# A Nyström attention with a SiLU layer behind it, on one core: landmarks spread in another slot, second-layer matmuls ahead of two groups of scores, batch 3's maximum by VectorE, and the first period and a load of v reordered

## The chip, the cores and the metric

The kernel runs on one core of a Trainium2 chip. The metric is the device time of one execution in microseconds. It uses TensorE (PE in the profile), VectorE (DVE), ScalarE (ACT), GpSimd (POOL) and SyncE (SP, which only issues DMAs here). GpSimd issues the loads of q, k, v and of both weights; SyncE issues the output stores and the DMA transposes.

## The reference

Eight batches, eight heads, 576 tokens, head size 64. q and k are averaged over 18 neighbouring tokens to 32 landmarks a head. Three softmax matrices are made, a pseudo-inverse of the middle one is iterated, and the product goes through a two-layer network with SiLU:

```python
def sm(a, b):
    s = scale * np.matmul(a, b.transpose(0, 1, 3, 2))
    s = s - np.max(s, axis=-1, keepdims=True)
    e = np.exp(s)
    return e / (np.sum(e, axis=-1, keepdims=True) + 1e-09)
A = sm(q, k_lm)
Bm = sm(q_lm, k_lm)
C = sm(q_lm, k)
Z = Bm.transpose(0, 1, 3, 2) / (norm1(Bm) * norminf(Bm) + 1e-06)
for _ in range(6):
    Z = 2 * Z - Z @ Bm @ Z
attn = A @ Z @ C @ v
x = attn, heads side by side: (4608, 512)
h = x @ w_in                      # 512 to 2048
g = h * (1.0 / (1.0 + np.exp(-h)))
out = g @ w_out                   # 2048 to 512
```

## The kernel before

The order of the work is written out by hand: each engine runs its instructions in the order of the program, and waits only on semaphores.

**Loops.** After a prologue that does batch 0's attention, an outer loop goes over the batches b = 0 to 7, one "period" each. Within it run 16 slots, s = 0 to 15. In every slot TensorE does one step of the first layer for batch b (`l1`, four matmuls into a PSUM tile `hps`), ScalarE applies SiLU to it and writes `gT` (`act`), and TensorE then does some matmuls of the second layer (`l2_mm(n)`, group `ops`, 512 columns each, 16 to a tile of 128 tokens), from a queue of finished token tiles. How many is listed by slot: `CNT[0]` and `CNT[1]` for loops 0 and 1, `REST` for loops 2 to 7. Each period needs 72 of them. Whenever 16 are done, ScalarE copies the tile to `ost` and SyncE stores it.

**Attention of the next batch.** Between these steps loop b does the attention of batch b+1 (object `a` of class `Att`; `a0` is that of batch b). It starts in slot d, which is 2, 3, 0 for loops 0, 1 and the rest. The methods that matter here:

- `lm_t` (line 251): VectorE transposes the landmarks `lmn` to `lmc`. `bd_expand` (line 259): four GpSimd copies spread the landmarks of k from `lmc` into the block-diagonal `bd`, which A's scores read. `transpose_qk` (line 185): VectorE transposes one quarter of q and k to `qkT`; the scores read it. `landmarks_pool` (line 211 on): GpSimd sums the landmarks of batch b+2 in slots 4 and 8 of loops 2 to 5.
- `a_scores(i)`: TensorE makes A's scores for token chunks 2i and 2i+1 into a PSUM bank `sa`. `a_max(i)` (line 568): VectorE takes the maximum of each row and head, `nm`.
- Two ways to take off the maximum. Where `sub` is set (batches 4 to 7), `a_sub(i)` (line 581) has VectorE write `xs` = scores - maximum to SBUF, and one exponential, `a_exp_all` (line 589), does all five chunks. Elsewhere `a_shift(i)` has TensorE add the maximum to the scores in PSUM by one matmul, and `a_exp(i)` (line 594) does the exponentials from PSUM in three parts.
- `b_scores`, `b_max`, `b_exp` for the 32 by 32 matrix in `bb`; `c_scores`, `c_max`, `c_exp` for C in two banks `scp`. These two come from the same two PSUM buffers as `hps`, so that a first-layer step after C waits until the exponential or the activation before it has read its buffer.
- `f_mm`, `b_scale`, `f_out`, `ns_mm`, `ns_step`, `x_out`: the iteration for Z. `w_mm` (reads v and the transposed exponentials of C), `z_mm`, then `m_unit` or `m_pair`: the product with w_in, copied to `mb`, which the first layer of the next loop reads.

`psa` (tiles `sa`, `mp`, `atp`, `wp`, `zt`) has one bank, `pso` (`ops`, `mp`, `ctp` and others) two, `psh` (`hps`, `scp`, `mpp`) two tiles of two banks. ScalarE has to load another table to go from SiLU to the exponential and back (line 151); both changes lie in slots d+1 and d+2.

**The places of the change, before.** At the end of loops 2 to 5 slot 13 has an `m_pair` whose casts VectorE does, slot 14 the last `transpose_qk` and behind it `lm_t` and `bd_expand` for batch b+2. Slot 15 then makes that batch's first scores, maximum and subtraction, though their first reader comes one loop later:

```python
if s == (14 if b > 1 else 15):
    ready = Att(b + 2)
    ready.lm_t(0, 2)
    ready.bd_expand(0, 2, nc.gpsimd.tensor_copy)
if s == 15 and ready.sub:
    ready.a_first()
    ready.a_scores(0)
    ready.a_max(0)
    ready.a_sub(0)
```

In loop 0 the loads are issued in the order four blocks of `w_out`, then v of batch 1 in slot 0, then q and k of batch 2. The first token tile of the second layer starts in slot 4; its 16 matmuls read the four blocks of `w_out` in turn, four matmuls a block. v of batch 1 is read by `w_mm` in slot 8.

Of the kernel before, what the change touches and what calls it, by code (L numbers as in the profile page):

```python
# [40 lines left out]
def kernel(  # L41
# [9 lines left out]
    nc = tc.nc  # L51
    B, H, S, Dh = q.shape
    L = 32
# [55 lines left out]
    def load_v(b):  # L109
        vt = loadp.tile([VP, H, VC * Dh], BF, tag="v", name="v")  # L110
        nc.gpsimd.dma_start(out=vt, in_=v[b].rearrange("h (p c) d -> p h (c d)", c=VC))
        v_t[b] = vt
# [21 lines left out]
    def load_w_out(j):  # L134
        nc.gpsimd.dma_start(  # L135
            out=w_out_sb[:, 4 * j:4 * j + 4, :],
            in_=moe_w_out[512 * j:512 * j + 512, :].rearrange("(c p) m -> p c m", p=128))
# [88 lines left out]
    class Att:  # L226
        def __init__(self, b):
            self.b = b
            self.qkT, self.v, self.lmn = qkT_t[b], v_t[b], lmn_t[b]
            self.bd = bd_t[b % 2]  # L230


            self.tiled = b < 2
            self.by_dma = b >= 2

            self.sub = b >= 4

            self.mean = b <= 2

            self.split = SPLIT[b]  # L240
            self.lmc = attp.tile([128, 4, L, 2], BF, tag="lmc", name="lmc")
            self.bb = None
            self.m_done = 0
            self.csum = attp.tile([128, 2], FP, tag="csum", name="csum")
            self.eCT, self.t = [None, None], [None, None]
            self.s, self.sa, self.w = [None, None], [None] * 3, [None, None]
            self.fx = None
# [79 lines left out]
        def b_scale(self):  # L327
            cs = attp.tile([128, 2], FP, tag="cs", name="cs")
            nc.vector.tensor_reduce(out=cs, in_=self.bmt, op=OP.add, axis=AX.X)
            n1 = attp.tile([128, 2], FP, tag="n1", name="n1")  # L330
            nc.vector.tensor_reduce(out=n1, in_=cs.unsqueeze(2).to_broadcast((128, 2, L)),
                                    op=OP.max, axis=AX.X, apply_transpose=True)
            self.nrm = attp.tile([128, 2], FP, tag="nrm", name="nrm")
            w = self.fw
            self.fx = nsp.tile([128, 2, w + L], BF, tag=f"fx{w}", name="fx", bufs=3)
            if self.tiled:
                nc.vector.tensor_scalar(out=n1, in0=n1, scalar1=1e-6, scalar2=-1.0, op0=OP.add,
                                        op1=OP.mult)
                nc.vector.reciprocal(out=self.nrm, in_=n1)
                nc.vector.tensor_tensor(  # L340
                    out=self.fx[:, :, w:w + L], in0=self.bm,
                    in1=self.nrm.unsqueeze(2).to_broadcast((128, 2, L)), op=OP.mult)
                return
            nc.vector.tensor_scalar(out=n1, in0=n1, scalar1=1e-6, scalar2=None, op0=OP.add)
            nc.vector.reciprocal(out=self.nrm, in_=n1)
            for g in range(2):
                nc.vector.tensor_scalar(out=self.fx[:, g, w:w + L], in0=self.bm[:, g, :],
                                        scalar1=self.nrm[:, g:g + 1], scalar2=None, op0=OP.mult)
# [380 lines left out]
    def l2_mm(n):  # L729

        st = l2_state
        while n > 0 and st["queue"]:
# [16 lines left out]
                nc.sync.dma_start(out=out[r0:r0 + 128, :], in_=ost)  # L749


    CNT = {0: [0, 0, 0, 0, 4, 4, 4, 2, 4, 2, 2, 2, 2, 2, 2, 2],
           1: [2, 2, 2, 2, 2, 6, 8, 8] + [4, 3] * 4}
    REST = [4, 2, 14, 11, 3, 3, 3, 3, 4, 4, 4, 3, 4, 3, 4, 3]


    ORD = (1, 0, 3, 2)
# [8 lines left out]
    a = Att(0)  # L766
# [60 lines left out]
    a.ns_mm(last=True)  # L827
    a.x_out()
    load_w_out(2)
    load_w_out(3)  # L830
    at = ps2("atp")
    a.z_mm(at[:, 1, :])
# [13 lines left out]
    ready = None  # L846
    for b in range(B):
        nxt = b + 1 < B
        cnt = CNT.get(b, REST)
        h = {}  # L850
        a0 = a
        a, ready = ready, None
# [9 lines left out]
        for s in range(NDC):  # L862
# [3 lines left out]
            if s <= d and b < 2:  # L866
# [16 lines left out]
                if b == 0:  # L883
                    transpose_qk(1, ORD[s])
                    if s == 0:
                        load_v(1)
                        a = Att(1)
                    elif s == 1:
                        a.lm_t(0)
                else:  # L890
                    if s == 3:
                        landmarks_out(2, lp, 0, 4)
                        a = Att(2)
                        a.lm_t(0, 2)
                        a.bd_expand(0, 2, nc.gpsimd.tensor_copy)
                    transpose_qk(2, (1, 3, 0, 2)[s])
                l2_mm(cnt[s])
            elif not nxt or s == d:
# [1 line left out]
                act(s)  # L900
                l2_mm(cnt[s])
                if nxt and a.sub:
                    a.a_scores(1)
                    a.a_max(1)
                    a.a_sub(1)

            elif s == d + 1:
                l1(s)
                act(s)
                l2_mm(cnt[s])  # L910
                if b == 0:

                    transpose_qk(1, ORD[s])
                    a.lm_t(1)
                    a.bd_expand(0, 2, nc.gpsimd.tensor_copy)
                    for i in (1, 2):
                        a0.a_scores(i)
                        a0.a_max(i)
                a.b_scores()
                a.c_scores()  # L920
                if a.sub:
                    a.a_scores(2)
                a.b_max()
                a.c_max(0)
# [6 lines left out]
            elif s == d + 2 and a.sub:  # L931
                a.a_start()
                a.c_max(1)
                a.a_max(2)
                a.a_sub(2)
                a.c_exp(0)
                a.c_exp(1)
                a.a_exp_all()
                a.b_norm()
                l2_mm(cnt[s])  # L940
                table(AF.Silu)
                l1(s)
            elif s == d + 2:
                n = cnt[s]
# [19 lines left out]
                a.a_shift(2)  # L964
                a.a_exp(2)
                if b == 0:
                    a0.m_unit(2, nc.vector.tensor_copy, nc.scalar.copy)
                    a.f_mm()
                    a.b_scale()
                    a.f_out()  # L970
                    l2_mm(n)
                    a0.m_unit(3, nc.vector.tensor_copy, nc.vector.tensor_copy)
                else:
                    l2_mm(n - 4 - min(n - 4, 6))
                table(AF.Silu)
                l1(s)
            elif b == 0:
                l1(s)
                r = s - d
                if r == 3:  # L980
                    act(s - 1)
                    a.ns_mm()
                    a.c_transpose(0)
                    a.ns_step()
                    a.c_out(0, nc.scalar.copy)
                    a0.a_norm(1)
                    a0.a_norm(2)
                elif r == 4:
                    a.ns_mm()
                    a.c_transpose(1)  # L990
                    a.w_scale()
                    a.ns_step()
                    a.ns_mm()
                    a.c_out(1)
                    a.a_norm(0)
                    a0.a_transpose(1)
                    a0.a_out(nc.scalar.copy)
                elif r == 5:
                    a.ns_step()
                    a.ns_mm()  # L1000
                    a.a_norm(1)
                elif r == 6:
                    a.w_mm()
                    a.ns_step()
                    a.ns_mm()
                    a.w_out()
                    a.ns_step()
                    a.a_norm(2)
                elif r == 7:
                    a.ns_mm(last=True)  # L1010
                    a.x_out()
                    a.a_transpose(0)
                    a.a_out(nc.scalar.copy)
                elif r == 8:
                    a.z_mm(psa1("zt"))
                    a.z_out()
                    a.a_transpose(1)
                    a.a_out(nc.vector.tensor_copy)
                act(s)
                if r in (9, 11):  # L1020
                    a.m_pair(r - 9)
                l2_mm(cnt[s])
            elif s == d + 3:
                l1(s)
                act(s - 1)
# [49 lines left out]
            if b == 0:  # L1075
                if s == 4:
                    load_qk(2)
                elif s == 11:
                    load_qk(3)
                    load_v(2)  # L1080
            elif b + 2 < B:
                if s == (5 if b == 1 else 1) and b + 3 < B:
                    load_qk(b + 3)
                if s == 7 + d // 2:
                    load_v(b + 2)
                if s in (4 + d, 8 + d):
                    landmarks_pool(b + 2, (s - 4 - d) // 2)

                ts = (9, 10, 12, 14) if d == 0 else (10, 11, 12, 13)
                if s in ts:  # L1090
                    transpose_qk(b + 2, ORD[ts.index(s)])
                if s == (14 if b > 1 else 15):
                    ready = Att(b + 2)
                    ready.lm_t(0, 2)
                    ready.bd_expand(0, 2, nc.gpsimd.tensor_copy)
                if s == 15 and ready.sub:
                    ready.a_first()
                    ready.a_scores(0)
                    ready.a_max(0)
                    ready.a_sub(0)  # L1100
# [35 lines left out]
```

## Time and profile before

| what | value |
|---|---|
| median of three runs | 271.88 us (271.57 to 273.46) |
| profiled execution | 271.72 us, its span 269.9 us |
| TensorE busy | 256.3 us, 95% of the span |
| ScalarE busy | 172.6 us, 64% |
| VectorE busy | 159.7 us, 59% |
| GpSimd busy | 118.0 us, 44% |
| granted TensorE clock | 1.000 |
| second-layer matmuls (`ops`) | 576, 146.3 us |
| first-layer matmuls (`hps`) | 512, 82.5 us |

The span runs from the first instruction to the last; the rest of the execution's time lies around it. Loop 0 begins near 22.8 us, loop 1 near 54.5, loop 2 near 83.3, and each later one about 29.5 us after the one before; after loop 7 the last second-layer matmuls run from 254 to 266 us. In the rows of the timeline the columns are the start and the length in us, the engine, the line, the operation, the tiles written and read with their shapes, and in brackets how long the engine had been idle and what released it. An instruction's recorded length overlaps with its successor's on TensorE, so the rate is read from the starts or from the chain of waits.

### The profile page before, as it was taken

Reading aid. Unit: us, or ns where it says so; the run is one execution under the profiler, and the core shown is the slowest. Engines: PE = TensorE matmul, PEld = TensorE weight load, DVE = VectorE, ACT = ScalarE, POOL = GpSimd, SP = SyncE. Lnnn points to the kernel's source line nnn. Section 1 sums busy time; section 2 is a strip of 40 time slices with the busy share of each in tenths; the row PEclk is TensorE's granted clock in tenths of the full one; section 3 lists DMA queues with packets and bytes.
Section 4 is the critical chain, followed back from the end, with each engine's and each line's share of the span. In section 5 each row is a group of like instructions: output and inputs, shape, how many; then the busy total and the mean of one; then the engine's idle time right before and its main releaser. Section 6 shows DMA issues by size and latency. Waiting matters only on the chain.

```text
span 269.9 us, 6751 instructions
## 1 busy us (share of the span) xinstructions
PE 256.3 (95%) x2761; PEld 144.5 (54%) x2761; DVE 159.7 (59%) x392; ACT 172.6 (64%) x319; POOL 118.0 (44%) x169
## 2 busy tenths in 40 slices
PE   6899898999999999999998999899999999999994
PEld 2647554475555565555645565455545565555541
DVE  4768893549596767586785678586777664000000
ACT  2367966759648856678475956687576857635511
POOL 8515426114897089535964289308950030100000
PEclk9999999999999999999999999999999999999999
DMA  6999999965994955679197918213481612121122
GB/s 101 202 209 207 207 206 219 206 120 97 218 108 88 210 119 77 136 134 180 23 135 138 210 61 122 88 32 107 52 163 39 101 53 71 39 80 39 39 78 78
DMA packets 37790, 32.34 MB, mean 120 GB/s; under 512 B 18816, under 2 KB 29056, under 8 KB 37760
## 3 DMA queue, kind: packets, MB, share of 16 engines
q0 software_dynamic: 15104, 18.35, 42.2%
q1 hardware_dynamic: 22656, 13.57, 21.8%
q8 instruction: 21, 0.34, 0.5%
q14 instruction: 9, 0.07, 0.1%
HBM read 36.70 MB, written 9.44 MB: 171 GB/s over the span
## 4 chain that ended last, share of the span: by engine, by line
PE 75%; DMA 9%; DVE 8%; POOL 3%; issue 2%; ACT 1%; POOLq 0%; ACTq 0%
PE ops L77 41%; PE hps L77 20%; DMA v<-in_v_dram 7%; PE sa L77 3%; PE bb L77 3%; PE scp L77 2%; DVE mb L687 2%; PE mp L77 2%; DMA nat<-in_q_dram 2%; DVE qkT L185 2%; POOL bd L259 2%; PE lmp L77 1%; PE wp L77 1%; DVE nm L568 1%; POOL w_out_sb L135 1%
## 5 line engine op out<-in xcount | busy, mean ns | idle before, releaser
L77 PE MATMUL ops<-w_out_sb,gT 128*128 128x512 bf16 x576 | 146.3, 379 | 0.0
L721 ACT ACTIVATE gT<-hps 128x576 bf16<-128x576 f32 (+2 forms) x128 | 82.5, 650 | 61.8 <-PE hps L77 60.8
L77 PE MATMUL hps<-AT,mb 128*128 128x288 bf16 (+2 forms) x512 | 82.5, 286 | 0.0
L77 PEld LDWEIGHTS <-gT 128*128 128x128 bf16 x576 | 53.0, 98 | 47.1 <-issue 5.4
L77 PEld LDWEIGHTS <-mb 128*128 128x128 bf16 x512 | 48.0, 98 | 24.3 <-issue 0.9
L185 DVE STREAM_TRANSPOSE qkT<-nat 128x576 f32<-128x576 f32 x32 | 39.1, 1245 | 1.5 <-DMA nat<-in_k_dram 1.1
L620 POOL TENSOR_TENSOR an<-ex,arec 128x512 bf16<-128x512 bf16 (+2 forms) x24 | 21.1, 902 | 21.4 <-DVE arec L610 17.9
L747 ACT COPY ost<-ops 128x512 f32<-128x512 f32 x36 | 21.0, 584 | 13.7 <-PE ops L77 13.5
L384 DVE SCALAR_TENSOR_TENSOR fx<-fx,bb 128x320 bf16<-128x320 bf16 (+1 forms) x39 | 17.1, 438 | 18.0 <-PE bb L77 17.3
L211 POOL TENSOR_TENSOR lma<-nat 128x1152 f32<-128x1152 bf16 x10 | 23.7, 2374 | 0.0
L687 DVE CAST mb<-mp 128x512 bf16<-128x512 f32 x28 | 18.0, 685 | 9.7 <-PE mp L77 9.5
L151 ACT ACT_TABLE_LOAD x16 | 20.5, 1283 | 1.1 <-PEq L1120 0.8
L1033 POOL CAST gate<-fx 128x2 f32<-128x2 bf16 x6 | 1.1, 187 | 45.6 <-DVE fx L354 45.6
L568 DVE TENSOR_REDUCE nm<-sa 128x16 bf16<-128x512 f32 (+2 forms) x21 | 12.7, 622 | 11.2 <-PE sa L77 11.1
L259 POOL COPY bd<-lmc 32x128 bf16<-32x128 bf16 (+1 forms) x32 | 8.9, 279 | 21.6 <-DVE lmc L251 15.6
L77 PEld LDWEIGHTS <-qkT 128*128 128x128 bf16 (+1 forms) x160 | 9.9, 98 | 9.7 <-issue 5.7
L77 PEld LDWEIGHTS <-fx 32*32 32x32 bf16 (+1 forms) x168 | 8.3, 93 | 12.0 <-DVE fx L384 1.8
L688 ACT CAST mb<-mpp 128x1024 bf16<-128x1024 f32 x14 | 14.2, 1011 | 0.6 <-PE mpp L77 0.6
L77 PE MATMUL sa<-bd,qkT 128*128 128x128 bf16 (+1 forms) x148 | 11.7, 220 | 2.9 <-POOL bd L259 2.2
L605 DVE TENSOR_REDUCE arec<-ex 128x16 f32<-128x512 bf16 (+2 forms) x24 | 14.1, 587 | 0.1
L77 PE MATMUL bb<-fx 32*32 32x64 bf16 (+2 forms) x168 | 13.1, 205 | 0.4
L425 DVE TENSOR_REDUCE cmx<-scp 128x1 f32<-128x576 f32 x16 | 11.9, 753 | 1.0 <-PE scp L77 0.7
(110 smaller groups left out, 259.1 us busy)
## 6 DMA issues: line engine op xcount, KB each, us to landing
out_dram<-ost SPq DMA_DIRECT2D x36, 256.0 KB, 2.3
nat<-in_k_dram POOLq DMA_DIRECT2D x16, 288.0 KB, 6.5
nat<-in_q_dram POOLq DMA_DIRECT2D x16, 288.0 KB, 7.8
v<-in_v_dram POOLq DMA_DIRECT2D x8, 576.0 KB, 7.2
w_in_sb<-in_moe_w_in_dram POOLq DMA_DIRECT2D x4, 512.0 KB, 15.8
w_out_sb<-in_moe_w_out_dram POOLq DMA_DIRECT2D x4, 512.0 KB, 14.5
AT<-an SPq DMA_TRANSPOSE x30, 4.2
eCT<-eC SPq DMA_TRANSPOSE x12, 4.3
```

Of the source, the lines that this page charges most:

```text
L77: nc.tensor.matmul(out=o, lhsT=lhsT, rhs=rhs, start=start, stop=stop, skip_group_check=True)
L151: nc.scalar.activation(out=spare[:, 1:2], in_=spare[:, 0:1], func=func)
L185: nc.vector.transpose(out=o.rearrange("p (l t) -> p t l", t=SEG), in_=nat_t[b][:, j, :].bitcast(FP).rearrange("p (t l) -> p t l", l=L))
L211: nc.gpsimd.tensor_tensor(out=a1, in0=nat[:, :, 0:3 * w], in1=nat[:, :, 3 * w:6 * w], op=OP.add)
L259: copy[h % len(copy)](out=self.bd[p, g:g + n, 32 * h:32 * h + 32, :], in_=self.lmc[p].rearrange("p (g j) l e -> p g j l e", j=2)[:, g:g + ...
L384: nc.vector.scalar_tensor_tensor(out=n, in0=self.fx, scalar=2.0, in1=self.p, op0=OP.mult, op1=OP.add if self.tiled else OP.subtract)
L568: eng.tensor_reduce(out=self.nm[0:pr, c:c + n, :], in_=self.sa[i][0:pr, 0:256 * n].rearrange("p (c h l) -> p c h l", h=8, l=L), op=OP.max, ...
L620: nc.gpsimd.tensor_tensor(out=self.an[0:pr, c:c + n, :].rearrange("p c (h l) -> p (c h) l", l=L), in0=x, in1=r.unsqueeze(2).to_broadcast(( ...
L687: nc.vector.tensor_copy(out=o[:, r, 0:512], in_=m[r])
L688: nc.scalar.copy(out=o[:, :, 512:1024], in_=m2)
L721: nc.scalar.activation(out=gT_t[b][:, 2 * s:2 * s + 2, o + c0:o + c1], in_=h[:, :, 0:c1 - c0], func=AF.Silu)
L747: nc.scalar.copy(out=ost, in_=st["ps"])
```

## The change

It has five parts.

- In loops 2 to 5, `Att(b+2)`, `lm_t` and `bd_expand` move from slot 14, behind the last transpose, to slot 13, ahead of it.
- `REST` puts more second-layer matmuls ahead of A's second scores (5 for 4) and ahead of B's and C's scores (4 for 2), and fewer behind (12 for 14, 10 for 11).
- Batch 3 now has `sub`: VectorE takes its maximum off. A new flag `early` keeps for batches 4 to 7 what is done in the loop before; batch 3's three groups of scores, maxima and subtractions stand in slots 0, 1 and 2 of loop 2, the last behind the first four second-layer matmuls of slot 2.
- In loop 0, slot 4, the four second-layer matmuls come first, then `f_mm` with `b_scale` ahead of it, then `m_unit(2)` and `m_unit(3)`, one right behind the other. In slot 10 the two second-layer matmuls move ahead of `a_transpose(1)`. `CNT[0]` takes two matmuls out of slot 6 and puts two into slot 9.
- The load of v for batch 1 is issued between the third and the fourth block of `w_out`.

```diff
-            self.sub = b >= 4
+            self.sub = b >= 3
+
+            self.early = b >= 4
...
-            w = self.fw
+            w = self.fw = L if self.tiled else 128
...
-    CNT = {0: [0, 0, 0, 0, 4, 4, 4, 2, 4, 2, 2, 2, 2, 2, 2, 2],
+    CNT = {0: [0, 0, 0, 0, 4, 4, 2, 2, 4, 4, 2, 2, 2, 2, 2, 2],
            1: [2, 2, 2, 2, 2, 6, 8, 8] + [4, 3] * 4}
-    REST = [4, 2, 14, 11, 3, 3, 3, 3, 4, 4, 4, 3, 4, 3, 4, 3]
+    REST = [5, 4, 12, 10, 3, 3, 3, 3, 4, 4, 4, 3, 4, 3, 4, 3]
...
     load_w_out(2)
+    load_v(1)
     load_w_out(3)
...
                     if s == 0:
-                        load_v(1)
                         a = Att(1)
...
                 if nxt and a.sub:
-                    a.a_scores(1)
-                    a.a_max(1)
-                    a.a_sub(1)
+                    i = 1 if a.early else 0
+                    if i == 0:
+                        a.a_first()
+                    a.a_scores(i)
+                    a.a_max(i)
+                    a.a_sub(i)
 
             elif s == d + 1:
                 l1(s)
                 act(s)
                 l2_mm(cnt[s])
+                if a.sub and not a.early:
+                    a.a_scores(1)
+                    a.a_max(1)
+                    a.a_sub(1)
...
                 a.b_scores()
                 a.c_scores()
-                if a.sub:
+                if a.early:
                     a.a_scores(2)
...
             elif s == d + 2 and a.sub:
                 a.a_start()
                 a.c_max(1)
+                if not a.early:
+                    l2_mm(4)
+                    a.a_scores(2)
                 a.a_max(2)
                 a.a_sub(2)
...
-                l2_mm(cnt[s])
+                l2_mm(cnt[s] if a.early else cnt[s] - 4)
                 table(AF.Silu)
                 l1(s)
...
                 if b == 0:
+                    a.b_scale()
+                    l2_mm(n)
+                    a.f_mm()
+                    a.f_out()
                     a0.m_unit(2, nc.vector.tensor_copy, nc.scalar.copy)
-                    a.f_mm()
-                    a.b_scale()
-                    a.f_out()
-                    l2_mm(n)
                     a0.m_unit(3, nc.vector.tensor_copy, nc.vector.tensor_copy)
...
                 elif r == 8:
                     a.z_mm(psa1("zt"))
                     a.z_out()
+                    l2_mm(cnt[s])
                     a.a_transpose(1)
...
-                l2_mm(cnt[s])
+                l2_mm(cnt[s] if r != 8 else 0)
...
+                if s == 13 and b > 1:
+                    ready = Att(b + 2)
+                    ready.lm_t(0, 2)
+                    ready.bd_expand(0, 2, nc.gpsimd.tensor_copy)
                 ts = (9, 10, 12, 14) if d == 0 else (10, 11, 12, 13)
                 if s in ts:
                     transpose_qk(b + 2, ORD[ts.index(s)])
-                if s == (14 if b > 1 else 15):
+                if s == 15 and b == 1:
                     ready = Att(b + 2)
                     ready.lm_t(0, 2)
                     ready.bd_expand(0, 2, nc.gpsimd.tensor_copy)
-                if s == 15 and ready.sub:
+                if s == 15 and ready.early:
                     ready.a_first()
                     ready.a_scores(0)
```

## The prediction

> **What bounds the kernel now.** I read first the page's busy times and its two lines of slices, then the list of waits, then the timeline around each place that the diff touches. A stretch over one batch period says who sets the pace:
>
> ```profile
> PE 256.3 (95%) x2761; PEld 144.5 (54%) x2761; DVE 159.7 (59%) x392; ACT 172.6 (64%) x319; POOL 118.0 (44%) x169
> PEclk9999999999999999999999999999999999999999
> 114.40:143.90 29.50, 28.79 (x304) 16.21 (x301) 21.40 (x50) 20.11 (x35) 18.48 (x25) 1.00 0.75 120
> ```
>
> TensorE is busy 28.79 of 29.50 us at full clock. It takes its instructions in order, so nothing but its own work and its own idle gaps counts. The waits name the gaps:
>
> ```profile
> PE sa L77 <- POOL bd L259: 2.2, 4, 0.6
> PE sa L77 <- DVE xs L581: 0.6, 4, 0.2
> PE wp L77 <- DMA v<-in_v_dram: 0.5, 1, 0.5
> ```
>
> The first two occur once in each of four periods, the third once, in the first period. One of the four, around 114 us (columns: start, length):
>
> ```profile
> 112.41 0.28 DVE L251 STREAM_TRANSPOSE lmc<-lmn 128x128 f32<-128x128 f32 x1
> 112.70 0.81 PE L77 MATMUL ops<-w_out_sb,gT 128*128 128x512 bf16 x3
> 112.75 1.27 POOL L259 COPY bd<-lmc 32x128 bf16<-32x128 bf16 x4 [2.79 <-DVE lmc L251]
> 114.07 0.62 PE L77 MATMUL sa<-bd,qkT 128*128 128x128 bf16 x8 [0.56 <-POOL bd L259]
> 115.02 1.03 PE L77 MATMUL ops<-w_out_sb,gT 128*128 128x512 bf16 x4
> 115.45 0.69 DVE L581 TENSOR_TENSOR xs<-sa,nm 128x512 f32<-128x512 f32 x1
> 116.20 0.64 PE L77 MATMUL sa<-bd,qkT 128*128 128x128 bf16 x8 [0.16 <-DVE xs L581]
> 118.93 3.18 PE L77 MATMUL ops<-w_out_sb,gT 128*128 128x512 bf16 x14
> 121.39 1.28 ACT L589 ACTIVATE ex<-xs 128x1280 bf16<-128x1280 f32 x1
> 124.56 1.17 ACT L721 ACTIVATE gT<-hps 128x576 bf16<-128x576 f32 x2
> 125.56 0.65 PE L77 MATMUL hps<-AT,mb 128*128 128x288 bf16 x4
> ```
>
> An "ops" matmul takes 0.216 us (fourteen advance the chain by 3.02). Three from 112.70 end at 113.35; A's first scores start at 114.07, 0.72 late, 0.05 after the last bd copy. Four from 115.02 end at 115.88; A's second scores start at 116.20, 0.32 late, because their one PSUM bank is free only when xs ends at 116.14.
>
> **Part a, the landmarks spread in slot 13.** Transpose and four copies (0.28 + 1.27 us) now stand ahead of the last q/k transpose (1.25 us) instead of behind it. VectorE ends its casts of mb in slot 13 at 111.40, so lmc is ready at 111.6, bd at 112.95 and the transpose at 112.8, both before 113.35. The copies now run beside a transpose. The trace has this: at 61.05 four copies took 1.28 us while a transpose at 60.85 took 1.22. GpSimd's queue has nothing between (its landmark sums end at 109.96; the loads of the next period stay behind). All 0.72 goes, four times: -2.9. If the cover is gone: 0.
>
> **Part b, the new counts in loops 3 to 6.** Loops 2 to 7 get 5, 4, 12 and 10 second-layer matmuls in slots 0 to 3 instead of 4, 2, 14 and 11: no work more or less. Take the moment of A's first scores as T (114.07 above). One more ahead of A's second scores fills 0.22 of the 0.32; they stay at T+2.13. Two more ahead of B's and C's scores put these 0.43 later, less the 0.13 that the second score bank now waits for a Silu activation: 0.30. Two fewer behind make the next first-layer step 0.13 earlier, one fewer after that puts the step of slot 4 at 125.56 - 0.13 - 0.22 = 125.21, which is 0.35 gained, if its PSUM bank is free. That bank is freed by the activation that starts at 124.56 and ends 0.65 later, at 125.21. ScalarE works without a pause up to it, from the exponentials through two table loads. Queued behind C's later scores are VectorE's maxima and the last subtraction: xs ends at 121.29 + 0.30 = 121.59, so the big exponential starts at 121.64 instead of 121.39, and with it the output copy, the table load and the activation come 0.25 later: 125.46. The step then starts at 125.50 instead of 125.56. I take -0.06 a batch, -0.2 in four, and keep -0.35 a batch (ScalarE not late) and +0.2 (twice as late) as ends: -1.4 to +0.8. In loop 7 no scores stand between; 0.
>
> **Part c, batch 3's maximum by VectorE (loop 2).** Gone are three TensorE matmuls that add the shift (0.216, 0.216 and 0.11 us by their columns: 0.54); three exponentials (1.57) become one of 1.28. New are three subtractions by VectorE (0.69, 0.69, 0.42). A's first scores move from behind C's scores to slot 0. In before the period runs so:
>
> ```profile
> 84.33 1.03 PE L77 MATMUL ops<-w_out_sb,gT 128*128 128x512 bf16 x4
> 94.68 1.17 ACT L721 ACTIVATE gT<-hps 128x576 bf16<-128x576 f32 x2
> 96.04 0.65 PE L77 MATMUL hps<-AT,mb 128*128 128x288 bf16 x4
> ```
>
> Five "ops" from 84.33 put T at 85.41 (bd is there at 84.96). From T on VectorE does what it does in the four later batches: maximum, subtraction, maximum, subtraction (to T+4.2), B's and C's maxima, maximum, subtraction (to T+7.2), as 121.29 stands to 114.07. The big exponential starts then, and the activation that frees the bank ends 3.8 later, at T+11.1, as 125.21 stands to 114.07. That is 96.5; the step starts at 96.55 instead of 96.04. TensorE itself would be there at about 95.6, so its saving of 0.54 ends in a wait of about 0.9 us. C's exponentials, and SP's transposes of them, come about 2.4 us later too; at the page's 4.3 us to landing they are there by 97, and w, their reader, came at 99.17. I take +0.5. Ends: -0.5 if ScalarE were no limit, +1.2 if its whole delay (94.68 to 95.9) came through.
>
> **Part d, the first period.** The page's queue of weights and v is served in order of issue, about 2.5 us each: the four w_out blocks are issued at 20.44 to 22.71 and land at 32.26 to 39.88 (11.8 and 17.2 us on), v, issued at 23.52, lands 19.3 later at 42.8. With v ahead of the last w_out block, v lands at 40.3 and the block at 42.8. The block's first reader is the 13th second-layer matmul; the counts 4, 4, 2, 2, 4 put that into slot 8, behind w.
>
> ```profile
> 33.34 0.22 PE L77 MATMUL bb<-bmt 32*32 32x32 bf16 x8 [0.34 <-ACT ex L594]
> 36.27 0.49 PE L450 MATMUL ctp<-ident,eC 128*96 128x128 bf16 x6 [0.26 <-DVE mb L667]
> 42.85 0.56 PE L77 MATMUL wp<-v,eCT 96*32 96x64 bf16 x48 [0.50 <-DMA v<-in_v_dram]
> 47.27 0.64 PE L642 MATMUL atp<-ident,an 128*128 128x128 bf16 x4 [0.45 <-DVE zwT L518]
> ```
>
> Slot 4: the four "ops" now fill the wait for the exponentials, f keeps its start at 33.34 (it reads the bank that they release), and both m units come behind it at 33.49. But the second of them waits for the copies of the first, done at 34.63, where before it stood behind the "ops": it ends at 35.0 instead of 34.8, and C's transpose comes at 36.48 instead of 36.27. So 0.2 is lost, and slots 5 to 7 run 0.2 late with two "ops" fewer (0.43). w then starts at 41.9, its v long there, ends at 42.4, and the "ops" behind wait for the w_out block: 42.86, against 43.51 before, with two still owed in slot 9: 0.65 - 0.43 = 0.2 gained. In slot 10 two "ops" now stand in the 0.6 us between z and A's transpose; that hides 0.5. Sum -0.7; ends -1.2 (both waits gone, nothing lost) and +0.3 (the lost 0.2, a late block, nothing hidden).
>
> **Sum.** The profiled execution took 271.72 us (span 269.9, 1.8 around it), 0.16 under the median of the runs. -2.9 - 0.2 + 0.5 - 0.7 = -3.3; 271.88 - 3.3 = 268.6, rounded to **268.5**.
>
> **Rivals.**
>
> *ScalarE's chain costs more.* In loops 2 to 6 my step of slot 4 hangs on an estimate of VectorE's and ScalarE's queue to a tenth. For it: two table loads of 1.28 us lie in it, and b starts with no slack. Against it: ScalarE is only 64% busy and has room after. At 0.4 us more in each of five: 270.5.
>
> *TensorE alone sets it.* If exponentials and activations keep up, b gives 1.4 and c gives 0.5 instead of costing it: 271.88 - 2.9 - 1.4 - 0.5 - 0.7 = 266.4. Against it: the activations at 124.56 have no idle time named before them.
>
> *GpSimd and VectorE shut each other out, slower than before.* The bd copies start just as the last transpose would, in slots 13 and 14. If the copies hold the transpose back until 112.95, it ends at 114.2, and A's first scores, which need it too, start at 114.25 instead of 114.07: a turns from -2.9 into +0.7, and the sum is 272.2. It decides from 0.55 us of delay (112.8 to 113.35) on. Against it: the overlapping copies and transpose at 61 us were as long as alone, and a cast at 83.75 too. The Trainium skill, "SBUF — State Buffer", section "Who interferes with whom", knows such an exclusive lock between the two engines, which would give this time; it names copies, casts and scalar forms in two-port modes and operations with two SBUF inputs, and an operation with one input outside those modes is said not to contend. By that the transposes are safe, and the trace's 1.22 us agrees.
>
> *The move does nothing*, since the scores also need the last transpose: they would wait for it at 112.8, still before 113.35; part of the lock's chance.
>
> **How the numbers follow.** Forecast 0.60 (267.6 to 269.6), ScalarE's chain 0.19, TensorE alone 0.14, lock 0.07. The range 266.8 to 270.5 leaves out half of TensorE alone, half of ScalarE's chain and the lock, 0.2 or a little more. About 1%, 2.7 us, is what a measurement of this kernel can tell from no change; that line is 269.2. Faster by more: 0.14 and most of the forecast, 0.66. Slower by more than 1% needs the lock and ScalarE's chain together: 0.04. The rest: 0.30.
>
> **What would show it.** Right: no wait of sa for bd; sa's second wait near 0.1; first-layer steps of slot 4 waiting for an activation, about 0.9 us in loop 2 and 0.3 in loops 3 to 6; no wait of w for v, and one of "ops" for a w_out block at 42.8; periods of loops 3 to 5 near 28.7 us instead of 29.5. Wrong: bd or the transposes longer than 1.3 us, a wait of sa for qkT, or a period unchanged though sa no longer waits.

## The result, and the profile after

The changed kernel takes **269.38 us** (median of 6 runs, 268.52 to 270.85), the kernel before 272.19 in the 6 runs beside it: a ratio of 0.990, with a 95% interval of 0.9865 to 0.9935. Forecast were 268.5, and 266.8 to 270.5 as the range. The profiled execution took 269.39 us, its span is 267.4.

The page's line of busy times, and the same stretch as before, one period of loop 3 (columns: length, then busy time and instructions of PE, PEld, DVE, ACT and POOL, the clock, the share and rate of the DMAs):

```profile
PE 250.0 (93%) x2718; PEld 143.4 (54%) x2758; DVE 161.6 (60%) x395; ACT 173.4 (65%) x317; POOL 118.0 (44%) x169
```

```profile
114.00:142.74 28.74, 28.04 (x300) 16.15 (x302) 21.46 (x50) 20.24 (x35) 19.08 (x26) 1.00 0.80 133
```

The period is 28.74 us instead of 29.50, at the same clock, and TensorE still fills it. (Its total on the page is lower than it was, but the trace of this execution holds 2718 matmuls beside 2758 weight loads, so some forty are missing and the totals are not to be subtracted; the lengths of periods are.) The list of waits has lost its entry of "sa" for "bd" and that of "wp" for v. Of the two lines below the first is nearly the same as before, the second is new:

```profile
PEld L77 <- DVE xs L583: 2.7, 6, 0.6
PE hps L77 <- ACT gT L723: 2.1, 5, 0.7
```

The second line says that five times in the run a first-layer step waits for an activation, 0.7 us at most. (The step of slot 3 in loop 2 also waits, 0.20 us, for an exponential of C.) The first is a weight load that waits ahead of A's scores; it stands beside matmuls that are still running, so most of its 2.7 us costs nothing. The timeline around the beginning of loop 3 (columns: start, length; the line numbers are two higher than before):

```profile
111.64 0.30 DVE L253 STREAM_TRANSPOSE lmc<-lmn 128x128 f32<-128x128 f32 x1
111.86 1.22 DVE L185 STREAM_TRANSPOSE qkT<-nat 128x576 f32<-128x576 f32 x1
112.00 1.27 POOL L261 COPY bd<-lmc 32x128 bf16<-32x128 bf16 x4 [1.78 <-DVE lmc L253]
113.67 0.62 PE L77 MATMUL sa<-bd,qkT 128*128 128x128 bf16 x8
115.06 0.69 DVE L583 TENSOR_TENSOR xs<-sa,nm 128x512 f32<-128x512 f32 x1
115.80 0.64 PE L77 MATMUL sa<-bd,qkT 128*128 128x128 bf16 x8
121.25 1.27 ACT L591 ACTIVATE ex<-xs 128x1280 bf16<-128x1280 f32 x1
124.42 1.17 ACT L723 ACTIVATE gT<-hps 128x576 bf16<-128x576 f32 x2
125.10 0.65 PE L77 MATMUL hps<-AT,mb 128*128 128x288 bf16 x4 [0.27 <-ACT gT L723]
```

The copies of bd now run beside the last transpose, end at 113.27, and A's first scores at 113.67 wait for nothing. The second still start 2.13 after the first, as before, because their bank is free only when xs ends at 115.75; but the matmul that was put ahead of them now fills that wait up to about 0.1 us, too little for a bracket in the list. Further on the step of slot 4 waits 0.27 us, until the first of the two activations at 124.42 has given its bank back.

**Where the time went.** Below is the time from loop to loop, from the first-layer step of slot 0 to the next one, in the profiled execution of every kernel of this study. "Start" is the first of these steps, the end of the prologue; after loop 7's start every kernel takes 38.5.

| kernel | start | loop 0 | 1 | 2 | 3 | 4 | 5 | 6 | span |
|---|---|---|---|---|---|---|---|---|---|
| before | 22.76 | 31.73 | 29.34 | 30.70 | 29.52 | 29.52 | 29.53 | 28.34 | 269.9 |
| after | 23.49 | 30.96 | 29.34 | 30.34 | 28.73 | 28.73 | 28.73 | 28.54 | 267.4 |
| part a alone | 24.07 | 31.15 | 29.34 | 29.97 | 28.80 | 28.81 | 28.81 | 28.34 | 267.8 |
| without part c | 24.14 | 31.27 | 29.71 | 29.98 | 28.73 | 28.73 | 28.73 | 28.27 | 268.1 |
| part d alone | 23.25 | 30.97 | 29.34 | 30.70 | 29.53 | 29.53 | 29.53 | 28.33 | 269.7 |
| C's scores sooner | 23.27 | 30.97 | 29.34 | 30.34 | 28.59 | 28.59 | 28.58 | 28.31 | 266.5 |
| best version | 22.70 | 30.65 | 29.34 | 29.97 | 28.59 | 28.59 | 28.59 | 28.13 | 265.1 |
| batch 3's first scores sooner | 22.77 | 30.96 | 29.34 | 30.06 | 28.73 | 28.73 | 28.73 | 28.55 | 266.4 |
| two copies added | 22.92 | 30.96 | 29.34 | 30.35 | 28.73 | 28.73 | 28.74 | 28.27 | 266.6 |

In the kernel before loop 2 begins at 83.83, so half a microsecond after the 83.3 given above. From before to after the loops give -0.77, 0, -0.36, -0.79, -0.79, -0.80 and +0.20, in all -3.3. The start takes 0.73 back, so the two spans differ by 2.5 only.

### The profile page after: what moved, and what is told of

The parts are those of the page before. It is cut to its first block, busy times and chain, and to the rows that moved or that the text cites. A ratio compares the mean times of both kernels' runs of the same rounds, so it can differ in the third digit from the quotient of the medians.

```text
span 267.4 us, 6703 instructions
## 1 busy us (share of the span) xinstructions
PE 250.0 (93%) x2718; PEld 143.4 (54%) x2758; DVE 161.6 (60%) x395; ACT 173.4 (65%) x317; POOL 118.0 (44%) x169
## 3 DMA queue, kind: packets, MB, share of 16 engines
q1 hardware_dynamic: 22656, 13.57, 22.4%
## 4 chain that ended last, share of the span: by engine, by line
PE 77%; ACT 7%; DVE 6%; issue 4%; DMA 3%; POOL 1%; POOLq 0%; ACTq 0%; DVEq 0%
PE ops L77 39%; PE hps L77 23%; DMA nat<-in_q_dram 3%; ACT L151 3%; PE bb L77 3%; PE sa L77 3%; PE mp L77 2%; PE lmp L77 2%; DVE cmx L427 2%; PE wp L77 1%; PE scp L77 1%; ACT gT L723 1%; PE mpp L77 1%; DVE nm L570 1%; ACT ost L749 1%
## 5 line engine op out<-in xcount | busy, mean ns | idle before, releaser
L77 PE MATMUL ops<-w_out_sb,gT 128*128 128x512 bf16 x540 | 138.9, 379 | 3.3 <-issue 2.2
L77 PE MATMUL sa<-bd,qkT 128*128 128x128 bf16 (+1 forms) x152 | 12.3, 220 | 0.2 <-DVE xs L583 0.2
```

The costliest lines, as they stand in the source:

```text
L77: nc.tensor.matmul(out=o, lhsT=lhsT, rhs=rhs, start=start, stop=stop, skip_group_check=True)
```

## Experiments

Kernels of one comparison ran beside the kernel before on the same chip: the first four beside a median of 272.37 us, batch 3's first scores and the best version beside 272.41.

### Part a alone: the landmarks spread in slot 13

```diff
 (kernel before)
+                if s == 13 and b > 1:
+                    ready = Att(b + 2)
+                    ready.lm_t(0, 2)
+                    ready.bd_expand(0, 2, nc.gpsimd.tensor_copy)
                 ts = (9, 10, 12, 14) if d == 0 else (10, 11, 12, 13)
...
-                if s == (14 if b > 1 else 15):
+                if s == 15 and b == 1:
```

> The kernel before with part a alone: transpose of the landmarks and the four bd copies in slot 13. Theory (TensorE's own idle gap was the whole price): each of loops 2 to 5 becomes 0.72 us shorter, A's first scores of slot 15 follow the matmul ahead of them without a wait, everything after them keeps its distance; 2.9 us less in all, ratio 0.989. Rival (given back later: A's second scores, which wait for VectorE's subtraction, or ScalarE's chain behind them wait longer once the first are early): the distance from A's first scores to the first-layer step of slot 4 grows over 11.5 us and less than 2 us are left.

Measured: 269.12 us, ratio 0.9877 (0.9856 to 0.9899). Loops 2 to 5 are 0.73, 0.72, 0.71 and 0.72 shorter than before, loop 6 is unchanged. So this part alone is worth 2.9 us, and A's second scores keep their late start (0.16 of wait, as before). By the medians part a alone can't be told from the whole change (0.9877 and 0.990, with intervals that overlap); the loops of the profiles tell them apart. The start of this profile is 1.31 later than before's; without it the span would be 3.4 shorter than before's instead of 2.1. Loop 0 is 0.58 shorter with not a line of it changed: everything up to slot 8 came later, so that v had landed (42.97) when w was to read it (43.59).

### The change without part c: batch 3's maximum as before

```diff
 (changed kernel)
-            self.sub = b >= 3
+            self.sub = b >= 4
...
-           1: [2, 2, 2, 2, 2, 6, 8, 8] + [4, 3] * 4}
+           1: [2, 2, 2, 2, 2, 6, 8, 8] + [4, 3] * 4,
+           2: [4, 2, 14, 11, 3, 3, 3, 3, 4, 4, 4, 3, 4, 3, 4, 3]}
```

> The changed kernel without part c: batch 3's maximum is again taken off by TensorE's shift matmuls, and loop 2 has its old counts 4, 2, 14, 11. Theory (in loop 2 ScalarE's chain sets the first-layer step of slot 4, so the 0.54 us of TensorE work saved is lost in a wait): loop 2 up to that step becomes about 0.37 us shorter than in the changed kernel, with no wait for an activation there, and the whole 0.4 us faster. Rival (TensorE's work sets the pace): 0.54 us longer.

Measured: 268.23 us, ratio 0.9842 (0.9819 to 0.9866). Loop 2 takes 29.98 instead of 30.34, and the step of slot 4 comes 12.20 after its start instead of 12.58. So part c costs 0.36. (The edit puts back loop 2's counts as well, so this is the price of both; "batch 3's first scores sooner" below gets 0.28 of it back by the place of two matmuls alone.) The two timelines at that step, with part c:

```profile
95.68 1.17 ACT L723 ACTIVATE gT<-hps 128x576 bf16<-128x576 f32 x2
96.36 0.65 PE L77 MATMUL hps<-AT,mb 128*128 128x288 bf16 x4 [0.71 <-ACT gT L723]
```

and without it:

```profile
95.97 1.17 ACT L723 ACTIVATE gT<-hps 128x576 bf16<-128x576 f32 x2
97.32 0.65 PE L77 MATMUL hps<-AT,mb 128*128 128x288 bf16 x4
```

With part c the first activation ends when the step begins, and TensorE has stood for 0.71. Without it the activations start 1.35 ahead of the step and nothing waits. TensorE has more to do there, the three matmuls for the shift, and yet is done sooner.

### Part d alone: the first period

The kernel before with all edits of loop 0 (counts, the load of v between w_out's third and fourth block, the orders of slots 4 and 10) and no other. With `b_scale` ahead of `f_mm` goes one line that sets `self.fw` there, to the value that `f_mm` has set so far.

```diff
 (kernel before)
-    CNT = {0: [0, 0, 0, 0, 4, 4, 4, 2, 4, 2, 2, 2, 2, 2, 2, 2],
+    CNT = {0: [0, 0, 0, 0, 4, 4, 2, 2, 4, 4, 2, 2, 2, 2, 2, 2],
...
     load_w_out(2)
+    load_v(1)
     load_w_out(3)
...
```

> The kernel before with part d alone: loop 0's order, its counts and the load of v. Theory (slot 8 is bound by the last block of weights, which lands at about 42.9 us whatever stands ahead): the second-layer matmuls of slot 8 wait for that block if TensorE gets there before 42.9; loop 1 starts 0.5 to 0.75 us earlier than in the kernel before, all later loops are as long as before. If the q and k loads of the first microseconds land late, as they did by 0.7 us in the profile of the changed kernel, loop 1 starts at the same time all the same, without that wait. Rival (the gain is work, not a wait on a transfer): a late start moves loop 1 by as much.

Measured: 271.60 us, ratio 0.9969 (0.9954 to 0.9984). Loop 0 takes 30.97 instead of 31.73, and nothing else moves. The theory had loop 1 start at the same time after a late start; it doesn't. Loop 0 has the same length whatever the start, 30.96 or 30.97 in five of the six profiles with these edits, and loop 1 moves with the start, as the rival said. What the edits gain does depend on the start: against the 31.15 of the old order after the late start of "part a alone" only 0.18 would be left, as there v had landed in time anyway.

The sixth profile, without part c, shows 31.27. In it the granted TensorE clock was 0.50 for 3.41 us around the start of loop 0:

```profile
21.32:24.73 3.41, 3.41 (x33) 2.63 (x32) 2.06 (x4) 0.98 (x4) 3.13 (x5) 0.50 1.16 208
```

Slot 0, from 24.14 to 25.30, takes 1.17 there and 0.87 in the eight others; that is the whole difference. The 0.37 more in its loop 1 lie in slot 9, in code that is the same: w waits there for a DMA transpose of C's exponentials that landed at 74.83, 7.8 us after its issue (7.1 to 7.5 in the others).

```profile
74.88 0.36 PE L77 MATMUL wp<-v,eCT 96*32 96x64 bf16 x24 [0.22 <-DMA eCT<-eC]
```

### Slots 0 to 3 with C's scores not delayed

```diff
 (changed kernel)
-    REST = [5, 4, 12, 10, 3, 3, 3, 3, 4, 4, 4, 3, 4, 3, 4, 3]
+    REST = [5, 2, 14, 10, 3, 3, 3, 3, 4, 4, 4, 3, 4, 3, 4, 3]
...
+           2: [5, 4, 12, 10, 3, 3, 3, 3, 4, 4, 4, 3, 4, 3, 4, 3]}
```

Loop 2 keeps the counts of the changed kernel.

> The changed kernel with the counts 5, 2, 14, 10 in loops 3 to 7: the two second-layer matmuls that part b put ahead of B's and C's scores go back behind them; loop 2 keeps 5, 4, 12, 10. Theory (ScalarE's chain, started by C's scores, frees the bank of the first-layer step in slot 4): the chain starts 0.3 us sooner, that step comes about 11.27 us after A's first scores instead of 11.43, its wait shrinks from 0.44 to under 0.15, and loops 3 to 6 get 0.6 to 0.9 us shorter in all. Rival (TensorE's work and the wait of the second score bank set it): the step comes 0.13 us later a loop and 0.5 us are lost.

Measured: 268.96 us, ratio 0.9878 (0.9843 to 0.9912); that interval holds the changed kernel's ratio, the profile resolves the effect. The fifth matmul ahead of A's second scores stays, the two ahead of B's and C's go back. Loops 3 to 5 take 28.59 instead of 28.73. The same three places as in the changed kernel's timeline of loop 3, which there had 121.25, 124.42 and 125.10:

```profile
120.79 1.28 ACT L591 ACTIVATE ex<-xs 128x1280 bf16<-128x1280 f32 x1
123.97 1.17 ACT L723 ACTIVATE gT<-hps 128x576 bf16<-128x576 f32 x2
124.74 0.65 PE L77 MATMUL hps<-AT,mb 128*128 128x288 bf16 x4
```

The loop began at 113.92 here and at 114.13 there. Counted from that, the exponential is 0.25 earlier, the activations 0.24, and the step 0.15, without a wait. That is ScalarE's chain moving with C's scores as the prediction had it, from the other side.

### Batch 3's first scores sooner

```diff
 (changed kernel, slot 0)
-                l2_mm(cnt[s])
+                late = 2 if nxt and a.sub and not a.early else 0
+                l2_mm(cnt[s] - late)
...
                     a.a_sub(i)
+                l2_mm(late)
```

> The changed kernel, only that in slot 0 of loop 2 two of the five second-layer matmuls (2 x 0.213 = 0.43) are issued behind batch 3's first scores instead of ahead of them; its expanded landmark matrix is ready since 84.96, the scores start at 85.56. Theory (in slot 4 of loop 2 the first-layer step waits for ScalarE's chain, which hangs on these scores): the step of slot 4 comes 0.3 to 0.43 sooner, its wait of 0.71 stays, loop 2 gets back to 29.9 to 30.0 from 30.34, and the time is 0.3 to 0.4 below the changed kernel's. Rival (the chain hangs on VectorE's work behind the second and third scores, or on the landmark work of the next batch): the first scores come sooner, the step of slot 4 does not, its wait grows by nothing and loop 2 stays at 30.3. It also shows whether loop 6's late exponential (0.24 to 0.38 late in the two profiles where batch 3's maximum is on VectorE, in no other) comes a third time.

Measured: 268.51 us, ratio 0.9865 (0.9842 to 0.9888). Loop 2 takes 30.06 instead of 30.34, the step of slot 4 comes 12.30 after its start instead of 12.58.

```profile
84.28 0.62 PE L77 MATMUL sa<-bd,qkT 128*128 128x128 bf16 x8
86.53 0.62 PE L77 MATMUL sa<-bd,qkT 128*128 128x128 bf16 x8
95.38 0.65 PE L77 MATMUL hps<-AT,mb 128*128 128x288 bf16 x4 [0.71 <-ACT gT L723]
```

The loop began at 83.08, so first scores, second scores and the step come at 1.20, 3.45 and 12.30; in the changed kernel, from 83.79, at 1.58 (85.37; the expectation has 85.56), 3.72 and 12.57. Of the 0.38 that the first scores gain, 0.27 reaches the second scores, whose wait for xs (0.16 on the timeline) is gone, and the same 0.27 arrives at the step. The wait of 0.71 is unchanged: the step hangs on the chain that begins at these scores, and between the second scores and the step nothing gave way. The gain is a little under the 0.3 to 0.43 that was expected, because from the second scores on TensorE's own order sets the pace of that chain.

### Two copies ahead of everything: loop 6

Loop 6 was the one place where the change made a period longer: 28.54 instead of 28.34, and 28.27 without part c. Its big exponential starts 0.24 after ScalarE is free, and 0.37 after its input xs is written (at 207.35); in the other loops it follows xs by 0.09:

```profile
206.93 0.42 DVE L583 TENSOR_TENSOR xs<-sa,nm 128x256 f32<-128x256 f32 x1
207.72 1.27 ACT L591 ACTIVATE ex<-xs 128x1280 bf16<-128x1280 f32 x1 [0.24 <-DVE bm L307]
211.57 0.65 PE L77 MATMUL hps<-AT,mb 128*128 128x288 bf16 x4 [0.55 <-ACT gT L723]
```

The releaser named there, bm, isn't read by the exponential. The same delay came in all three profiles with part c (this one, "C's scores sooner", "batch 3's first scores sooner"), in loop 6 and in no other loop, and in none of the kernels without part c. In those three the exponential of loop 6 has the same place in ScalarE's list, and part c makes that list two instructions shorter ahead of it.

```diff
 (changed kernel)
     idle(wt, 12, 512)
+    nc.scalar.copy(out=spare, in_=spare)
+    nc.scalar.copy(out=spare, in_=spare)
```

> The changed kernel with two small ScalarE copies (2 columns of a spare tile onto itself) added in the first microseconds, where ScalarE has nothing else to do; nothing else differs. In the three profiles with batch 3's maximum on VectorE, ScalarE's big exponential of loop 6 (ACT L591) starts 0.32 after the wait ahead of it has ended, in all other loops and kernels 0.04; it is the same place in ScalarE's list of instructions each time, two places ahead of the one that it has in the kernels without that edit. Theory (the delay belongs to a place in ScalarE's list, not to the data): with the list two instructions longer ahead of it, the exponential of loop 6 starts 0.04 behind its wait as in the other loops, the wait of slot 4's first-layer step there falls from 0.55 to about 0.27, loop 6 gets from 28.55 to 28.3, and the time moves by no more than 0.3. Rival (it is a late input of the exponential that goes with batch 3's edit): the delay of 0.3 is there again and loop 6 stays at 28.55.

Measured, in a single run: 268.26 us, beside 271.67 of the kernel before. In the profile:

```profile
206.38 0.43 DVE L583 TENSOR_TENSOR xs<-sa,nm 128x256 f32<-128x256 f32 x1
206.90 1.27 ACT L591 ACTIVATE ex<-xs 128x1280 bf16<-128x1280 f32 x1
210.75 0.65 PE L77 MATMUL hps<-AT,mb 128*128 128x288 bf16 x4 [0.27 <-ACT gT L723]
```

The exponential now starts 0.09 after xs, the step's wait is 0.27 instead of 0.55, loop 6 takes 28.27 instead of 28.54, and every other loop is unchanged. Two instructions that do nothing, two hundred microseconds earlier, take the delay away: it belonged to a place in ScalarE's list and not to the exponential's inputs. What happens at that place isn't shown, and stays open. The trace has one thing near it: in every kernel a transfer of the kind "instruction" on queue q14 begins soon after this exponential, 0.94 to 1.12 us after it in the three that have the delay (at 208.84 in the changed kernel) and 0.16 to 0.50 in the six others. So the fetching of instructions may be the cause; no run tests that, nor does the trace say whose instructions these are. The rest of the difference to the changed kernel's profile is the start, 22.92 instead of 23.49.

### The best version

Part a; batch 3's maximum left on the old way; counts 5, 2, 14, 10 in loops 3 to 7; of part d the load of v and the order of slot 10, with slot 4 as it was before, and the four second-layer matmuls of slot 8 moved to slots 9 and 10.

```diff
 (changed kernel)
-            self.sub = b >= 3
+            self.sub = b >= 4
...
-    CNT = {0: [0, 0, 0, 0, 4, 4, 2, 2, 4, 4, 2, 2, 2, 2, 2, 2],
-           1: [2, 2, 2, 2, 2, 6, 8, 8] + [4, 3] * 4}
-    REST = [5, 4, 12, 10, 3, 3, 3, 3, 4, 4, 4, 3, 4, 3, 4, 3]
+    CNT = {0: [0, 0, 0, 0, 4, 4, 2, 2, 0, 6, 4, 2, 2, 2, 2, 2],
+           1: [2, 2, 2, 2, 2, 6, 8, 8] + [4, 3] * 4,
+           2: [4, 2, 14, 11, 3, 3, 3, 3, 4, 4, 4, 3, 4, 3, 4, 3]}
+    REST = [5, 2, 14, 10, 3, 3, 3, 3, 4, 4, 4, 3, 4, 3, 4, 3]
...
                 if b == 0:
-                    a.b_scale()
-                    l2_mm(n)
+                    a0.m_unit(2, nc.vector.tensor_copy, nc.scalar.copy)
                     a.f_mm()
+                    a.b_scale()
                     a.f_out()
-                    a0.m_unit(2, nc.vector.tensor_copy, nc.scalar.copy)
+                    l2_mm(n)
```

> The changed kernel with three edits that the runs so far point to. (1) Batch 3's maximum goes back to GpSimd and loop 2 to its old counts (second run: loop 2 0.36 shorter). (2) Loops 3 to 7 issue 5, 2, 14 and 10 second-layer matmuls in slots 0 to 3 instead of 5, 4, 12 and 10 (fourth run: loops 3 to 5 0.15 each shorter). (3) Of the first period, slot 4 keeps the order of the kernel before, with m_unit(2) first, since the changed order made that slot 12.29 where it was 12.04; the load of v between w_out's third and fourth block and the order of slot 10 stay as changed, and slots 8 and 9 issue 0 and 6 second-layer matmuls instead of 4 and 4, so that nothing asks for the fourth w_out block before slot 9 (44.4; the block landed at 42.96). Expected: loop 2 0.36 shorter than in the changed kernel, loops 3 to 6 0.15 to 0.3 each, loop 0 0.25, together 1.3: 268.0 to 268.2, 0.984 of the kernel before. Rival (the gains of loop 0 are taken by the start, whose place moved by up to 1.3 between runs, and TensorE's list takes back half of the rest): 268.9. Loop 0's slots 4 to 8 tell edit (3) by itself: 12.04 in slot 4 if the order costs, 12.3 if it is the m_unit(3) pair that costs either way.

Measured: **267.07 us** (266.85 to 267.67), ratio 0.9807 (0.9787 to 0.9826), the whole interval below the changed kernel's. One period of loop 3:

```profile
112.66:141.25 28.59, 28.11 (x298) 16.25 (x301) 21.50 (x50) 20.00 (x35) 19.03 (x26) 1.00 0.79 132
```

Against the changed kernel: loop 0 -0.31, loop 2 -0.37, loops 3 to 5 -0.14 each, loop 6 -0.41 (0.27 of it the delay that goes with part c), in all 1.5 where 1.3 was expected, and 0.79 by the start. Of the 1 us that the median lies below the expected time the loops thus explain 0.2; for the rest only the start of the profiled execution is on record. In its list of waits no first-layer step waits for an activation any more. The step of slot 4 in loop 0 comes 12.03 after the start, as in the kernel before; with part d's order it came after 12.28.

## Why the prediction was right

It was right in place and mechanism, and its sum over the loops was nearer than the median tells: -3.3 forecast, -3.3 measured from loop 0 to loop 6 (that the two agree so closely is in part luck, since errors of its terms cancel). What is missing in the profiled execution lies ahead of the loops.

| step | forecast | measured |
|---|---|---|
| a, four times | -2.9 | -2.9 (part a alone) |
| b, loops 3 to 6 | -0.2 | -0.07, -0.08, -0.08 and, in loop 6, +0.20: -0.03 |
| c, loop 2 | +0.5 | +0.36 |
| d, loop 0 | -0.7 | -0.77 |
| start | 0 | +0.73 in this profile |

**Part a** went as written: copies of 1.27 us beside a transpose of 1.22, all of the 0.72 gone, four times. With that the lock between GpSimd and VectorE falls, and with it the rival that the move does nothing. The rule of the Trainium skill, "SBUF — State Buffer", section "Who interferes with whom", by which a VectorE operation with one SBUF input outside the two-port modes doesn't contend with GpSimd, agrees with these two durations; the section names no transposes.

**Part b** was followed to the hundredth. From A's first scores on (113.67) the exponential was to start at 7.57, the activation to end at 11.39 and the step to start at 11.43; they did at 7.58, 11.40 and 11.43. The -0.06 a batch came in loops 3 to 5, as -0.07 and -0.08. The step that failed is its fourth repetition: loop 6 was counted like the others, and is 0.27 longer by the delay of ScalarE that came with part c. The reasoning held in reverse, too: with C's scores not delayed the chain came 0.25 sooner, and the loop gained the 0.15 that TensorE allowed.

**Part c** was right in sign and in its cause, 0.14 too high. The chain from the first scores to the step was put at 11.1 us and took 10.99 (85.37 to 96.36), so the wait was 0.71 instead of 0.9. The rival "TensorE alone sets it" would have had a gain of 0.5 here, and the kernel without part c refutes it. It is worth seeing why the edit loses: it takes three matmuls from TensorE and gives the time to a chain through VectorE and ScalarE, at the one place of the loop where TensorE can't go on without that chain.

**Part d** has the right sum from terms that were partly wrong. The forecast was a slot 4 that loses 0.2, a w that no longer waits for v, "ops" behind it that wait for the w_out block until 42.86, and 0.5 hidden in slot 10. Slot 4 lost 0.25:

```profile
34.07 0.22 PE L77 MATMUL bb<-bmt 32*32 32x32 bf16 x8 [0.32 <-ACT ex L596]
35.43 0.41 PE L77 MATMUL mp<-w_in_sb,zwT 64*32 64x512 bf16 x8 [0.81 <-DVE mb L669]
42.82 0.56 PE L77 MATMUL wp<-v,eCT 96*32 96x64 bf16 x48
```

At 35.43 the second m unit waits for the copies of the first, as forecast, and w at 42.82 waits for nothing. But no "ops" ever waited for the block. In the profile of "batch 3's first scores sooner", whose start is before's to 0.01, w began at 42.10, eight matmuls of the iteration (`bb`) stood behind it, and the "ops" came at 42.76; the block had landed at 42.64. The step that was mis-sized is the 42.4 at which TensorE was to stand there: w came 0.2 later, and those eight matmuls, 0.17, were left out. So it missed a wait by 0.12 us, and slot 8 gained 0.57 where the forecast leaves 0.42 for it (0.65 in all from slot 4 on, with 0.2 lost and 0.43 of "ops" moved away ahead of it). Slots 9 and 10 take 3.89 where they took 3.91, with two "ops" more (0.43): 0.45 hidden, forecast 0.5.

**The start** was no step of the sum at all. The loops begin at 22.76 in the profile of before and at 23.49 in that of after, and nothing that runs before that was moved. The first loads landed later: the third of them at 9.22 instead of 8.60, the fourth at 11.01 instead of 10.04, and TensorE's second and third group of landmark sums started at 9.27 and 11.05 instead of 8.84 and 10.35. In the nine profiles the start lies between 22.70 and 24.14. In seven of them the granted clock was 1.00 up to there, and the start, 22.70 to 23.49, comes 12.5 to 12.9 after the fourth load's landing. The two latest, 24.07 (part a alone) and 24.14 (without part c), come 13.57 and 14.05 after it: each has 3.41 us at a clock of 0.50, from 7.44 and from 21.32 on.

In the profiled execution the start is most of the gap: its 269.39 lies 0.8 above 268.6, which is what the sum gives before it was put down as 268.5. That the median of six runs is the same 269.38 doesn't show that their starts were as late, for only this one has a profile. Against the 272.19 of the kernel before in the same comparison the median fell by 2.8, 0.5 less than the loops, and how much of that is the start stays open.

Of the range's other reasons, "ScalarE's chain costs more" wasn't met (0.4 more in each of five loops; it was 0.1 less in loop 2, the same in loops 3 to 5, and 0.27 more in loop 6 for another reason).

## What to carry to other kernels

Where TensorE is 95% busy, look for the few places where it can't go on without another engine, and count from one such place to the next; an edit that freed TensorE elsewhere in that stretch bought nothing here, and one that let the other engine's chain end later cost what that end then lay behind TensorE's own arrival (0.71 in loop 2, 0.27 in loops 3 to 5). Split a span at fixed marks before comparing two profiles, and read the granted clock of each part: a start that differs by 0.7 us from one execution to the next, three microseconds at half the clock, or a wait that vanishes because everything ahead came late, otherwise passes for the effect of an edit.

## What the runs showed of the hardware that was not expected

- One activation started 0.3 us late for no reason in its data. It started 0.37 to 0.39 us after its input was written in three kernels that have it at one place of ScalarE's list, 0.09 to 0.10 in all others and in the changed kernel with two instructions added ahead.
- With the same loads issued at the same moments (the first four at 1.32 to 3.14 us), the fourth landed at 9.90 to 11.01 in the nine profiles. In the seven that had the full clock ahead of the loops the first period began 22.70 to 23.49 us into the span.
- In the two other profiles the granted TensorE clock was 0.50 for 3.41 us near the beginning (7.44 to 10.85, and 21.32 to 24.73), though the mean of the whole execution is 0.992. Their first period began at 24.07 and 24.14.
